# Scores of the last 64 queries of two heads as four fp32 matmuls on 64x64 tiles, and a new order of all rounds

## The chip, the cores and the metric

The kernel runs on one core of one Trainium2 chip. The time is that of the device for one execution, in microseconds (us), as the median of the runs shown. Work is done by TensorE (PE in the rows; its weight loads are PEld), VectorE (DVE), ScalarE (ACT) and GpSimd (POOL); SyncE (SP) issues most of the DMAs. Each of them runs its own instructions in the order in which the program lists them, and waits where an operand or a buffer is not ready yet.

## What is computed

Attention with a bias that depends on the positions, and after it a feed-forward layer with a softplus. The shapes are B = 4, H = 8, S = 576, D = 64, and for the layer 2304 tokens, 512 columns in and out and 2048 hidden.

```python
def _attn_ref(q, k, v, w1, b1, w2):
    scores = np.matmul(q, k.transpose(0, 1, 3, 2)) / np.sqrt(D)
    rel = (pos[:, None] - pos[None, :]).astype(np.float32)
    x = (np.log1p(np.abs(rel)) / np.log1p(np.maximum(pos[:, None], 1.0)))[..., None]
    bias = np.maximum(x @ w1 + b1, 0.0) @ w2
    scores = scores + bias.transpose(2, 0, 1)[None]
    attn = np.exp(scores - np.max(scores, axis=-1, keepdims=True))
    attn = attn / (np.sum(attn, axis=-1, keepdims=True) + 1e-09)
    return np.matmul(attn, v)

def _moe_ref(x, w_in, w_out):
    h = x @ w_in
    return (np.maximum(h, 0.0) + np.log1p(np.exp(-np.abs(h)))) @ w_out
```

## The kernel before

The first part (to about 66 us) computes the bias tables of all heads and, between them, the scores of the first two units. A **unit** n (16 of them) is one batch element and a pair of heads; the second part works through them in **rounds** 0 to 15, and in round n it multiplies the probabilities of unit n with v, while it makes the scores of unit n+1 and splits the q and k of unit n+2. The third part (from about 320 us) is the feed-forward layer.

Two heads have 2 x 576 query rows, which make nine tiles of 128 rows: tiles 0 to 3 are of the first head, 5 to 8 of the second, and tile 4 holds the last 64 queries of both. q and k come into the tiles `qn` and `kn` (pool `nat`, two buffers each; `kn` holds k twice, once in each half of the partitions). VectorE or ScalarE round them to fp32r (`hi_q`, `hi_k`, into `qq` and `kk`), and GpSimd subtracts to get what the rounding left out (`lo_q`, `lo_k`). A tile's scores are four matmuls of 128x288: two halves of the keys, each with the high and the low part of k, and the contraction over 128 partitions adds the high and the low part of q. Tile 4 takes eight, because the two heads are added up in one accumulation: in `qq` 64 columns of zeros lie between the two heads' queries, so that the product of the other head's rows is zero.

The order within a round is written out by hand, in strings of tokens (`ROUND0`, `ROUND1`, `ROUND` for rounds 2 to 13, `ROUND14`, `ROUND15`). A token is an instruction group of one engine, and a letter behind a slash names the engine of a copy (a for ScalarE, d for VectorE):

- `S4` is the matmuls of the scores of tile 4 of unit n+1, into one of two PSUM buffers `s` in turn (`Z4` the same for unit n). `A4` adds the bias and finds the row's extreme, on VectorE, and frees the buffer. `X4` is the exponential with the row's sum, on ScalarE.
- `T31` is the transposes of part 1 of key block 3 of unit n, into one of two PSUM buffers `t` in turn (three transposes; `T40` two, of the key tail's copies `tl`). `V31` copies them to SBUF and frees the buffer. `L0` to `L4` make the tail copies, on GpSimd.
- `P0` to `P4` multiply key blocks 0 to 4 with v, on TensorE in fp32, where each matmul leaves two records in the trace. P0 to P3 use array tiles of 128x64, and P4, the key tail, four of 64x64. P3 and P4 of unit n-1 stand at the head of round n.
- `I` adds up and inverts the row sums, `R` transposes them, `C` copies them and sends them out to memory, from where they come back spread over 64 partitions (`rb`); `O` multiplies the product with them.
- `Kh`, `Qh0`, `Qh1` are the roundings of k and of the two heads' q, `Kl`, `Ql0`, `Ql1` the subtractions.
- `B0` to `B4` decode a block of the layer's weights: B0 on ScalarE, B1 on GpSimd, B2 to B4 on VectorE.

The loads (`LOADS`) are hung on the numbers of tokens in the round.

Of the kernel before, what the change touches and what calls it, by code (L numbers as in the profile page):

```python
# [42 lines left out]


ROUND = """
Qh1/d Kh/a P3 P4 T20 T02 S2 Qh0/a I V20/d V02/d T11 V11/a A2 S3 T12 V12/a T00 V00/a S7 A3 O T10
A7 V10/a S4 R Kl S0 X3 C B0 T41 T22 Ql1 V41/a A4 S1 V22/a B1 A0 Ql0 T30 V30/a S6 T01 T21 V01/a
X7 S5 A1 B2 X4 A6 V21/d T31 V31/d X2 S8 A8 T32 X0 A5 B3 X8 L0 V32/d X5 X1 T40 P0 L2 L1 P1 V40/d
L4 P2 X6 L3 B4
"""  # L50

ROUND0 = """
Z7 T20 T30 V20/a A1 A0 ZA7 V30/a ZX7 Z3 X1 A6 X0 Z4 ZA3 A2 Z8 T10 ZX3 ZA8 ZX8 T00 A5 V00/d ZL2
ZL1 V10/d T40 T12 T02 X6 V40/a V12/a A7 ZA4 X7 A3 V02/a T32 ZX4 V32/d T22 V22/a X2 I T01 R Qh1/d
ZL3 T31 ZL4 V01/a C A4 T11 X5 P0 Kh/a X4 V11/d Qh0/d L2 Ql0 Kl X3 L1 L4 A8 L0 P1 X8 V31/d T21 L3
V21/d T41 V41/d P2 Ql1
"""
# [64 lines left out]
def tile_log_bias_attention__then__softplus_ffn(  # L122
# [192 lines left out]
    def u_split(n):  # L315

        def hi_k(on="d"):
            kk[n] = kp.tile([128, 2, 2, S], F32R, tag="kk", name="kk")
# [6 lines left out]
        def hi_q(i, on="d"):  # L330
# [1 line left out]
            copy_on(on, qq[n % 2][up, 640 * i:640 * i + S], q_n[n][up])

        def lo_q(i):
            done.add(("q", n, i))
            qt = qq[n % 2][:, 640 * i:640 * i + S]
# [1 line left out]
            sub_on(n)(qt[down], q_n[n][up], qt[up], op=ALU.subtract)
# [24 lines left out]
    def u_s(n, t):  # L363

        pr, b = divmod(n, B)
        st_ = {}

        def pe():
            ssum[n] = sums[n % 3]
            if t == 4:  # L370
# [10 lines left out]
            if t < 4:  # L381
                terms = [(0, 128 * t)]
            elif t > 4:
                terms = [(1, 128 * t + 64)]
            else:
                terms = [(0, 512), (1, S)]
            for half in range(2):
                for i, (hd, c0) in enumerate(terms):
                    for j in range(2):
                        nc.tensor.matmul(  # L390
                            ps[:, half, :SH],
                            lhsT=qt[:, c0:c0 + 128],
                            rhs=kt[:, hd, j, half * SH:half * SH + SH],
                            start=(i == 0 and j == 0),
                            stop=(i == len(terms) - 1 and j == 1),
                        )
# [692 lines left out]
```

## Time and profile before

| | |
|---|---|
| time, median of 3 runs (lowest to highest) | 710.72 us (710.49 to 710.92) |
| the profiled execution | 713.52 us |
| its span, first to last instruction | 711.7 us |
| busy in the span: PE, PEld | 684.4 us, 538.2 us |
| busy in the span: DVE, ACT, POOL | 526.7 us, 532.6 us, 122.1 us |
| mean granted clock of TensorE | 0.990 |

The profiled execution took 1.8 us more than its span and 2.8 us more than the median. Steps are costed in its span; what they change is then taken from the median. A record of a matmul is longer than its place in the stream, because matmuls are pipelined: 288 columns show as some 295 ns, though the next one starts 133 ns later. How long TensorE is held is read from the distance between starts.

### The profile page before, as it was taken

To read this page: it belongs to the slowest core of one execution; us is meant where nothing else is said; L and a number is where in the kernel's file an instruction comes from. 1 tells how busy PE (TensorE), PEld (TensorE's weight loads), DVE (VectorE), ACT (ScalarE), POOL (GpSimd) and SP (SyncE) were. 2 spreads that over 40 slices of the span, in tenths; PEclk is the share of its full clock that TensorE was granted. 3 is DMA by queue.
4 is the path that set the end of the run, shared out by engine and by line. 5 is a ranking of instruction groups with operands and counts; after the bars stand their busy time and mean duration, and the time that the engine had idled before them with its cause. 6 is when DMAs were issued, how large, how long until landed. Compare 5 with 4: busy or idle time off the path is not lost.

```text
span 711.7 us, 11929 instructions
## 1 busy us (share of the span) xinstructions
PE 684.4 (96%) x4128; PEld 538.2 (76%) x4128; DVE 526.7 (74%) x1115; ACT 532.6 (75%) x1079; POOL 122.1 (17%) x150
## 2 busy tenths in 40 slices
PE   5689899999999999999999999999999999999997
PEld 2135588877888777757888888888888888888886
DVE  6996788887888887767968695678695554666464
ACT  6989788888888887778777686777677665665654
POOL 0000555455655454210000000000000000000000
PEclk9999899999999999999999999999999999999999
DMA  5866786677677543555232120512020220412221
GB/s 139 305 225 218 245 295 209 215 245 237 190 227 229 168 144 112 161 164 175 93 144 75 50 99 1 178 65 84 29 75 16 103 75 1 137 41 81 68 80 39
DMA packets 51036, 96.76 MB, mean 136 GB/s; under 512 B 7440, under 2 KB 15008, under 8 KB 50976
## 3 DMA queue, kind: packets, MB, share of 16 engines
q1 hardware_dynamic: 50460, 95.41, 41.0%
q8 instruction: 32, 0.52, 0.3%
q10 hardware_dynamic: 516, 0.60, 0.2%
q14 instruction: 28, 0.23, 0.1%
HBM read 67.98 MB, written 28.01 MB: 135 GB/s over the span
## 4 chain that ended last, share of the span: by engine, by line
PE 85%; ACT 5%; DMA 4%; DVE 4%; issue 1%; SPq 0%; ACTq 0%; POOL 0%; POOLq 0%; DVEq 0%
PE y L854 28%; PE h L796 27%; PE s L390 10%; PE o L504 10%; PE t L467 6%; PE acc L232 3%; DVE p L406 2%; DMA e_d<-e 2%; ACT p L422 2%; DVE b L689 1%; ACT e L253 1%; PE t L475 1%; DMA a<-w_d 1%; DMA r_d<-r 1%; DMA dist<-in_c_dist_dram 1%
## 5 line engine op out<-in xcount | busy, mean ns | idle before, releaser
L796 PE MATMUL h<-x,wi 128*128 128x512 f32 (+1 forms) x960 | 212.4, 370 | 1.1 <-DVE wi L769 1.1
L854 PE MATMUL y<-wo,g 128*128 128x512 f32 x864 | 209.8, 391 | 0.0
L796 PEld LDWEIGHTS h<-x,wi 128*128 128x128 f32 x960 | 169.1, 189 | 35.1 <-DVE wi L769 1.8
L854 PEld LDWEIGHTS y<-wo,g 128*128 128x128 f32 x864 | 161.2, 188 | 33.7 <-DVE g L828 0.2
L819 DVE SCALAR_TENSOR_TENSOR u<-u,e 128x512 f32<-128x512 f32 (+1 forms) x80 | 50.9, 637 | 102.3 <-ACT l L816 102.0
L390 PE MATMUL s<-kk,qq 128*128 128x288 f32 x640 | 118.0, 315 | 1.1 <-ACT p L400 0.2
L406 DVE CUSTOM_DVE_ANT_0 p<-s,b 128x576 f32<-128x576 f32 x135 | 99.5, 753 | 17.1 <-PE s L390 16.6
L422 ACT ACTIVATE p<-p,m 128x576 f32<-128x576 f32 x144 | 109.7, 765 | 3.1 <-DVE b L695 2.5
L812 ACT ACTIVATE e<-h 128x512 f32<-128x512 f32 (+1 forms) x80 | 44.2, 553 | 76.5 <-PE h L796 76.5
L390 PEld LDWEIGHTS s<-kk,qq 128*128 128x128 f32 x640 | 90.2, 191 | 9.6 <-DVE m L406 5.0
L467 PE MATMUL t<-ident,p 128*128 128x128 f32 x576 | 89.2, 280 | 1.8 <-ACT pt L355 1.6
L355 ACT ACTIVATE pt<-t 128x384 f32<-128x384 f32 (+1 forms) x126 | 58.3, 488 | 36.4 <-PE t L467 34.8
L504 PE MATMUL o<-pt,vn 128*64 128x256 f32 (+3 forms) x640 | 78.6, 416 | 0.0
L467 PEld LDWEIGHTS t<-ident,p 128*128 128x128 f32 x576 | 66.7, 142 | 14.3 <-issue 7.9
L504 PEld LDWEIGHTS o<-pt,vn 128*64 128x64 f32 (+1 forms) x640 | 38.9, 137 | 32.0 <-issue 5.7
L826 ACT ACTIVATE g<-l 128x512 fp32r<-128x512 f32 (+1 forms) x80 | 46.8, 586 | 20.4 <-DVE l L823 10.6
L357 DVE COPY pt<-t 128x384 f32<-128x384 f32 (+1 forms) x98 | 48.5, 530 | 15.8 <-PE t L467 15.6
L439 POOL COPY tl<-p 128x128 f32<-128x128 f32 x80 | 30.8, 399 | 146.2 <-ACT p L422 139.7
L232 PE MATMUL acc<-m,coef 128*32 128x512 f32 (+17 forms) x352 | 37.9, 528 | 17.6 <-ACT e L253 10.3
L828 DVE TENSOR_TENSOR g<-l,g 128x512 fp32r<-128x512 f32 (+1 forms) x80 | 50.3, 628 | 3.7 <-ACT g L826 3.7
L823 DVE TENSOR_TENSOR l<-l,u 128x512 f32<-128x512 f32 (+1 forms) x80 | 50.4, 630 | 0.0
L821 DVE SCALAR_TENSOR_TENSOR l<-h,l 128x512 f32<-128x512 f32 (+1 forms) x80 | 50.4, 630 | 0.0
(56 smaller groups left out, 686.1 us busy)
## 6 DMA issues: line engine op xcount, KB each, us to landing
e_d<-e SPq DMA_DIRECT2D x36, 295.5 KB, 5.0
kn<-in_k_dram SPq DMA_DIRECT2D x16, 576.0 KB, 4.9
b<-e_d SPq DMA_DIRECT2D x32, 288.0 KB, 4.4
r<-in_moe_w_in_dram SPq DMA_DIRECT2D x16, 512.0 KB, 3.5
r<-in_moe_w_out_dram SPq DMA_DIRECT2D x16, 512.0 KB, 3.6
xr<-x_d SPq DMA_DIRECT2D x28, 256.0 KB, 3.4
vn<-in_v_dram SPq DMA_DIRECT2D x16, 320.0 KB, 8.5
qn<-in_q_dram SPq DMA_DIRECT2D x16, 288.0 KB, 4.7
```

Of the source, the lines that this page charges most:

```text
L232: nc.tensor.matmul(acc[32 * g:32 * g + 32, lo:hi], lhsT=coef.rearrange("p o h -> p (o h)"), rhs=hid[s, g][:, lo:hi], start=True, stop=True ...
L355: nc.scalar.activation(dst, src, AF.Copy)
L390: nc.tensor.matmul(ps[:, half, :SH], lhsT=qt[:, c0:c0 + 128], rhs=kt[:, hd, j, half * SH:half * SH + SH], start=(i == 0 and j == 0), stop= ...
L406: nc.vector.tensor_tensor_reduce(prob[n, t].rearrange("p (a c) -> p a c", a=2), st_["ps"][:, :, :SH], bias[pr, t].rearrange("p (a c) -> p ...
L422: nc.scalar.activation(p, p, AF.Exp, bias=st_["m"], scale=-1.0, accum_out=ssum[n][:, PLACE.index(t):PLACE.index(t) + 1],)
L467: nc.tensor.transpose(ps[:, 128 * i:128 * i + 128], prob[n, t][:, 128 * jb:128 * jb + 128], ident,)
L504: nc.tensor.matmul(o[up, half, 0:w], lhsT=v_n[n][rows, jb, hd], rhs=pt[n, jb][rows, c0:c0 + w], start=(jb == 0), stop=(jb == 4), tile_posi ...
L796: nc.tensor.matmul(ps[:, :nb], lhsT=wi[f][:, a, 128 * c:128 * c + 128], rhs=xs[bi, c][:, x_, :nb], start=(i == 0), stop=(i == 11),)
L819: nc.vector.scalar_tensor_tensor(u, u, -1.0, e, op0=ALU.add, op1=ALU.subtract)
L821: nc.vector.scalar_tensor_tensor(l, ps, 0.0, l, op0=ALU.max, op1=ALU.add)
L823: nc.vector.tensor_tensor(l, l, u, op=ALU.subtract)
L854: nc.tensor.matmul(y, lhsT=g[:, a, 128 * ts:128 * ts + 128], rhs=wo[f][:, w_], start=(first and i == 0), stop=(last and i == 2),)
```

## The change

Tile 4 no longer uses the rounded parts. Its scores are four fp32 matmuls, one for each head and half of the keys, straight from `qn` and `kn`, each on an array tile of 64x64: the half of the keys chooses the half of the partitions, the head the half of the output's partitions. For that the host lays 64 more columns of q out (each half of the partitions then holds the last 64 queries of both heads), `qn` is 640 columns wide, the pool `nat` has three buffers, and the roundings and subtractions of q take 512 columns instead of 576. The zeros in `qq` are gone.

```diff
+            if t == 4:
+                for half in range(2):
+                    rows = slice(64 * half, 64 * half + 64)
+                    for hd in range(2):
+                        c0 = ((512, S), (S, 0))[hd][half]
+                        nc.tensor.matmul(
+                            ps[64 * hd:64 * hd + 64, half, :SH],
+                            lhsT=q_n[n][rows, c0:c0 + 64],
+                            rhs=k_n[n][rows, hd, half * SH:half * SH + SH],
+                            start=True,
+                            stop=True,
+                            tile_position=(64 * half, 64 * hd),
+                        )
+                return
...
-            else:
-                terms = [(0, 512), (1, S)]
...
-            copy_on(on, qq[n % 2][up, 640 * i:640 * i + S], q_n[n][up])
+            copy_on(on, qq[n % 2][up, 512 * i:512 * i + 512], q_n[n][up, 64 * i:64 * i + 512])
...
-                t = nat.tile([128, S], F32, tag="qn", name="qn")
+                t = nat.tile([128, S + 64], F32, tag="qn", name="qn")
...
+NAT = 3
...
-    nat = pool(es_s, "nat", 2, "right")
+    nat = pool(es_s, "nat", NAT, "right")
```

All the strings of tokens are new. In rounds 2 to 13 S4 now stands between P3 and P4; in round 1 it stands behind P4 and T20, and in round 14 between P3 and T20. K's rounding moves from ScalarE to VectorE (`Kh/a` to `Kh/d`) in rounds 2 to 13, and two more of the copies V go to ScalarE (10 of 14, from 8). The order of the loads is new, too. Line numbers shift by up to 14.

On TensorE, the head of a round in the middle of the attention, before: the products P2, P3 and P4 (two rows each), then T20 with T02, and the scores S2. `o` is the product's PSUM tile, `pt` the transposed probabilities, `vn` the values, `t` the PSUM tile of the transposes.

```order
L504 MATMUL o<-pt,vn 64x256 x2
L504 MATMUL o<-pt,vn 64x320 x2
L504 MATMUL o<-pt,vn 64x256 x2
L504 MATMUL o<-pt,vn 64x320 x2
L504 MATMUL o<-pt,vn 64x256 x2
L504 MATMUL o<-pt,vn 64x320 x2
L467 MATMUL t<-ident,p 128x128 x6
L390 MATMUL s<-kk,qq_126 128x288 x4
```

The same place after, with S4 as the row `s<-kn,qn`:

```order
L510 MATMUL o<-pt,vn 64x256 x2
L510 MATMUL o<-pt,vn 64x320 x2
L510 MATMUL o<-pt,vn 64x256 x2
L510 MATMUL o<-pt,vn 64x320 x2
L382 MATMUL s<-kn,qn 64x288 x4
L510 MATMUL o<-pt,vn 64x256 x2
L510 MATMUL o<-pt,vn 64x320 x2
L473 MATMUL t<-ident,p 128x128 x3
L396 MATMUL s<-kk,qq_125 128x288 x4
```

S4 moved to between P3 and P4, and S2 from behind T02 to ahead of it. On TensorE, the place in the middle of the round where S4 stood before: S7, T10, S4 (the row of eight), R (on `ss`, the sums), S0 and T41:

```order
L390 MATMUL s<-kk,qq_126 128x288 x4
L467 MATMUL t<-ident,p 128x128 x3
L390 MATMUL s<-kk,qq_126 128x288 x8
L556 MATMUL t<-ident,ss_128 128x128
L390 MATMUL s<-kk,qq_126 128x288 x4
L475 MATMUL t<-ident,tl 128x128 x3
```

The row of eight is gone from there; after, S7, R, S0 and T10 follow each other.

On VectorE, the last third of the same round, before: A1 (the first pair of rows; `p` the scores with the bias, `m` their extreme), B2 (`b<-a`), A6, the copies V21 and V31 (one row of two), A8, A5, B3 (`b<-r,b`) and V32:

```order
L406 ISA p,m<-s,b 128x576
L406 ISA m 128x1
L689 TENSOR_SCALAR b<-a 128x512
L406 ISA p,m<-s,b 128x576
L406 ISA m 128x1
L357 COPY pt<-t 128x384 x2
L406 ISA p,m<-s,b 128x576
L406 ISA m 128x1
L406 ISA p,m<-s,b 128x576
L406 ISA m 128x1
L695 SCALAR_TENSOR_TENSOR b<-r,b 128x512
L357 COPY pt<-t 128x384
```

The same stretch after, from V30 on: V30, A1, A6, B2, V31, A5, B3 and A8.

```order
L355 COPY pt<-t 128x384
L412 ISA p,m<-s,b 128x576
L412 ISA m 128x1
L412 ISA p,m<-s,b 128x576
L412 ISA m 128x1
L695 TENSOR_SCALAR b<-a 128x512
L355 COPY pt<-t 128x384
L412 ISA p,m<-s,b 128x576
L412 ISA m 128x1
L701 SCALAR_TENSOR_TENSOR b<-r,b 128x512
L412 ISA p,m<-s,b 128x576
L412 ISA m 128x1
```

A6 went ahead of B2. V30 came to VectorE from ScalarE, and V21 went the other way. V31 stands alone, behind A6 and B2. V32 is no longer in this stretch.

On VectorE, the stretch behind it, over the end of the round, before: B4 (`a<-r,b`), the rounding Qh1, the two steps of I (`ss`), and V20 and V02 of the next round:

```order
L700 SCALAR_TENSOR_TENSOR a<-r,b 128x512
L357 CAST qq_124<-qn 64x576
L542 TENSOR_SCALAR ss_128<-ss_128 128x9
L543 RECIPROCAL ss_128<-ss_128 128x9
L357 COPY pt<-t 128x384 x2
```

After: B4, V32, Qh1, Kh, the two steps of I, and A4:

```order
L706 SCALAR_TENSOR_TENSOR a<-r,b 128x512
L355 COPY pt<-t 128x384
L355 CAST qq_124<-qn 64x512
L355 CAST kk<-kn 128x2x576
L548 TENSOR_SCALAR ss_126<-ss_126 128x9
L549 RECIPROCAL ss_126<-ss_126 128x9
L412 ISA p_2307,m<-s,b 128x576
L412 ISA m 128x1
```

V32 is now the last copy of its round, behind B4. Kh came in from ScalarE, where it stood ahead of Qh0, and A4 follows I; V20 and V02 went to ScalarE.

## Rows read from the trace of the kernel before

**Rows 1.** Page, part 4: share of the span in the chain that ended last, by engine

```profile
PE 85%; ACT 5%; DMA 4%; DVE 4%; issue 1%; SPq 0%; ACTq 0%; POOL 0%; POOLq 0%; DVEq 0%
```

**Rows 2.** Busy time by window: length, each engine's busy us, granted clock, DMA share, GB/s

```profile
70.00:80.00 10.00, 7.18 (x35) 4.68 (x35) 7.60 (x21) 9.12 (x24) 1.63 (x4) 0.68 0.94 321
166.50:181.64 15.14, 15.08 (x125) 12.25 (x123) 12.84 (x32) 12.91 (x31) 8.11 (x9) 1.00 0.55 173
```

**Rows 3.** Timeline of PE, mid-round: start us, us, engine, line, operation, tiles, count

```profile
179.06 0.82 PE L467 MATMUL t<-ident,p 128*128 128x128 f32 x6
179.64 0.77 PE L390 MATMUL s<-kk,qq 128*128 128x288 f32 x4
180.25 0.49 PE L467 MATMUL t<-ident,p 128*128 128x128 f32 x3
180.49 1.31 PE L390 MATMUL s<-kk,qq 128*128 128x288 f32 x8
181.66 0.77 PE L390 MATMUL s<-kk,qq 128*128 128x288 f32 x4
```

**Rows 4.** Timeline of PE, end of the same round

```profile
184.89 0.77 PE L390 MATMUL s<-kk,qq 128*128 128x288 f32 x4
185.50 0.49 PE L467 MATMUL t<-ident,p 128*128 128x128 f32 x3
186.07 0.79 PE L390 MATMUL s<-kk,qq 128*128 128x288 f32 x4
```

**Rows 5.** Timeline of PE, products with v, passes taken one by one, then T20

```profile
173.45 0.39 PE L504 MATMUL o<-pt,vn 128*64 128x256 f32 x2
173.67 0.44 PE L504 MATMUL o<-pt,vn 128*64 128x320 f32 x2
173.94 0.44 PE L504 MATMUL o<-pt,vn 128*64 128x320 f32 x2
...
175.88 0.44 PE L504 MATMUL o<-pt,vn 128*64 128x320 f32 x2
176.24 0.50 PE L504 MATMUL o<-pt,vn 64*64 64x256 f32 x4
176.51 0.50 PE L504 MATMUL o<-pt,vn 64*64 64x256 f32 x4
176.94 0.87 PE L467 MATMUL t<-ident,p 128*128 128x128 f32 x6
```

**Rows 6.** Timeline of DVE, end of the same round: A1, B2, A6, V21 with V31

```profile
183.65 0.76 DVE L406 CUSTOM_DVE_ANT_0 p<-s,b 128x576 f32<-128x576 f32 x1 [0.37 <-PE s L390]
184.34 1.00 DVE L689 TENSOR_SCALAR b<-a 128x512 int32<-128x512 int32 x1
185.26 0.74 DVE L406 CUSTOM_DVE_ANT_0 p<-s,b 128x576 f32<-128x576 f32 x1
185.93 1.01 DVE L357 COPY pt<-t 128x384 f32<-128x384 f32 x2
```

**Rows 7.** Timeline of DVE, head of a round: B3, Qh1, V20 with V02

```profile
173.12 0.69 DVE L695 SCALAR_TENSOR_TENSOR b<-r,b 128x512 int32<-128x512 int32 x1
175.23 0.46 DVE L357 CAST qq<-qn 64x576 fp32r<-64x576 f32 x1
177.53 1.02 DVE L357 COPY pt<-t 128x384 f32<-128x384 f32 x2 [0.81 <-PE t L467]
```

**Rows 8.** Timelines of POOL and DVE, Kl, Qh1 and Ql1 in rounds 0, 1 and 7

```profile
81.96 2.64 POOL L328 TENSOR_TENSOR kk<-kn,kk 128x1152 fp32r<-128x1152 f32 x1
83.39 1.52 DVE L357 CAST qq<-qn 64x576 fp32r<-64x576 f32 x1
180.14 1.43 POOL L338 TENSOR_TENSOR qq<-qn,qq 64x576 fp32r<-64x576 f32 x1
```

**Rows 9.** Timeline of ACT, head of a round: the last X, then Kh

```profile
175.41 0.76 ACT L422 ACTIVATE p<-p,m 128x576 f32<-128x576 f32 x1
176.17 1.15 ACT L355 ACTIVATE kk<-kn 128x1152 fp32r<-128x1152 f32 x1
```

More of the change, by code (lines that the diff above doesn't have):

```diff
@@ L45 @@
 ROUND = """
[L46 to L49, printed above, removed]
+B0 Qh1/d Qh0/a P3 S4 P4 T20 V20/a S2 Kh/d T02 I A4 O A2 V02/a T12 S3 V12/a T11 A3 T00 S7 V11/a
+V00/d Ql0 R B1 S0 X3 C A7 T10 T41 A0 V10/a V41/a S1 T30 V30/d Kl A1 T22 X0 S6 V22/a T01 V01/a
@@ L50 @@
+T21 A6 V21/a S5 B2 T31 V31/d T32 S8 X7 T40 A5 B3 X4 V40/a X6 X1 X2 A8 P0 X5 X8 L0 B4 L2 L1 P1 L4
+L3 Ql1 V32/d P2
 """
 ROUND0 = """
[L53 to L56, printed above, removed]
+Z7 T20 T30 V30/a V20/a A1 A0 ZA7 ZX7 A6 X0 A2 Z3 Z4 ZA3 Z8 T10 ZX3 ZA8 ZX8 T00 A5 ZL1 T40 V00/d
@@ L57 @@
+V10/d ZL2 X1 A7 T12 T02 X6 ZA4 V40/a V12/a X7 A3 V02/a ZX4 T32 T22 V22/a V32/d I T01 R T11 ZL4
+V01/a ZL3 T31 C A4 Qh1/d X5 Kh/a X3 V11/d Qh0/d X4 X2 P0 Ql0 Kl A8 L0 P1 X8 L3 V31/d T21 V21/d
+L1 T41 V41/d P2 L4 Ql1 L2
 """
 ROUND1 = """
-Qh1/d Kh/a P3 P4 T20 Qh0/a I T02 S2 T11 V20/d V02/d V11/a A2 S3 T12 V12/a T00 V00/a S7 A3 O T10
-R Ql1 Kl X3 S4 S0 C V10/a T41 T22 B0 A7 V41/a A4 B1 S1 V22/a A0 Ql0 T30 T01 X4 V30/a V01/a S6 X7
-A1 S5 B2 A6 T21 V21/d T31 V31/d S8 A8 B3 T32 X0 A5 T40 X8 P0 X2 X5 X1 L2 X6 L0 L4 V40/d L3 P1 B4
@@ L63 @@
-P2 L1 V32/d
+Qh1/d Kh/a P3 P4 T20 S4 Qh0/a I T11 T02 S2 V20/d V02/d V11/a A4 A2 T12 S3 V12/a T00 V00/a S7 A3
+O T10 R Ql1 Kl X3 S0 V10/a C T41 T22 B0 A7 V41/d S1 V22/a A0 Ql0 T01 B1 X4 T30 V01/a S6 V30/a X7
+A1 B2 A6 S5 T21 V21/d T31 V31/d S8 A8 B3 T32 X0 A5 T40 X8 P0 X2 X5 X1 L0 L2 X6 L4 V40/d B4 P1 L3
+L1 V32/d P2
 """
 ROUND14 = """
-Qh0/d Kh/a P3 Qh1/d P4 I T20 T02 S2 V20/d V02/d T11 V11/a A2 S3 T12 V12/a T00 O V00/a S7 A3 T10
-A7 V10/a R S4 X3 C Kl B0 S0 T41 T22 Ql1 V41/a A4 S1 V22/a A0 T30 A1 V30/a B1 S6 T01 V01/a T21 B2
@@ L69 @@
-S5 A6 V21/d T31 X4 V31/d Ql0 X7 S8 X2 T32 X0 A5 A8 B3 X5 X1 L0 V32/d X8 T40 P0 V40/d P1 L2 X6 B4
-P2 L4 L3 L1
+Qh0/d Kh/a P3 I Qh1/d S4 T20 T02 P4 S2 V20/d A4 V02/d T11 V11/a A2 S3 T12 V12/a T00 O V00/a A3
+T10 S7 A7 V10/a R X3 C Kl B0 S0 T41 T22 Ql1 V41/d V22/a A0 S1 T30 A1 V30/a B1 S6 T01 T21 B2 S5
+A6 V21/d T31 V01/a X4 V31/d Ql0 S8 X7 X2 T32 B3 X0 A5 A8 X5 X1 L0 V32/d X8 T40 P0 V40/d P1 L2 X6
+L4 L3 L1 B4 P2
 """
 ROUND15 = """
-P3 I T00 V00/a T01 P4 T02 V02/a f2 T10 V01/d O R V10/d C T11 V11/a T12 V12/d P0 T32 f0 V32/a T20
@@ L75 @@
-V20/d T21 V21/d T22 P1 f7 T30 f4 f5 V22/a V30/d f3 T31 V31/a T40 f8 V40/a f9 T41 f1 V41/d f10
-f11 B0 P2 f6 B1 B2 B3 B4 f12
+P3 I T00 V00/a f2 T01 P4 V01/d T02 V02/a T10 O R V10/d C T11 V11/a T12 V12/d P0 T32 f0 V32/a T20
+V20/d T22 T21 V21/d P1 f7 T30 f4 f5 V22/a V30/d f3 T31 V31/a T40 f8 V40/a f9 T41 f1 V41/d f10
+f11 B0 P2 B1 f6 B2 B3 B4 f12
 """
@@ L95 @@
 LAG_S = (1, 4)
-LOADS = {30: "b", 2: "k", 6: "q", 10: "v", 14: "b", 18: "b", 22: "b", 26: "b", 40: "w"}
-LOADS0 = {74: "w", 14: "k", 35: "v1", 56: "v", 4: "q"}
+LOADS = {22: "b", 4: "q", 0: "v", 34: "w", 6: "k", 25: "b", 23: "b", 10: "b", 31: "b"}
+LOADS0 = {17: "k", 28: "v1", 71: "w", 6: "q", 59: "v"}
 PRE = [(f, i) for f in range(8) for i in range(2)][:15]
@@ L115 @@
 STAGE = """
-21:D00 22:R15 25:R10 25:R16 26:R12 26:D01 27:D05 29:R17 31:R11 32:D02 33:R13 33:D06 33:R18
+21:D00 21:R15 24:R16 25:R10 26:R12 26:D01 27:D05 29:R17 31:R11 31:R13 32:D02 33:D06 33:R18
 34:R14
@@ L262, in tile_log_bias_attention__then__softplus_ffn @@
     N = 16
-    QW = S + 64 + S
     qq = []
     for i in range(2):
-        t = sp.tile([128, QW], F32R, name=f"qq{i}")
-        nc.gpsimd.memset(t[:, S:S + 64].bitcast(F32), 0.0)
-        qq.append(t)
+        qq.append(sp.tile([128, 1024], F32R, name=f"qq{i}"))
     sums = [sp.tile([128, 128], F32, name=f"ss{i}") for i in range(3)]
@@ L331, in hi_q @@
             up = slice(64 * i, 64 * i + 64)
[L332 removed]
+            copy_on(on, qq[n % 2][up, 512 * i:512 * i + 512], q_n[n][up, 64 * i:64 * i + 512])
         def lo_q(i):
             done.add(("q", n, i))
[L336 removed]
+            qt = qq[n % 2][:, 512 * i:512 * i + 512]
             up, down = slice(64 * i, 64 * i + 64), slice(64 - 64 * i, 128 - 64 * i)
[L338 removed]
+            sub_on(n)(qt[down], q_n[n][up, 64 * i:64 * i + 512], qt[up], op=ALU.subtract)
         return hi_k, lo_k, hi_q, lo_q
@@ L378, in pe @@
             st_["ps"] = ps
+            if t == 4:
[12 more added lines that the diff above has]
+                return
             assert all(("q", n, i) in done for i in range(3))
             qt, kt = qq[n % 2], kk[n]
[L381 to L384, printed above, removed]
-            else:
-                terms = [(0, 512), (1, S)]
-            for half in range(2):
[L388 to L396, printed above, removed]
+            hd, c0 = (0, 128 * t) if t < 4 else (1, 128 * t - 128)
+            for half in range(2):
+                for j in range(2):
+                    nc.tensor.matmul(
+                        ps[:, half, :SH],
+                        lhsT=qt[:, c0:c0 + 128],
+                        rhs=kt[:, hd, j, half * SH:half * SH + SH],
+                        start=(j == 0),
+                        stop=(j == 1),
+                    )
         def raw():
@@ L1043, in _lay @@
         else:
-            a[:, 1::2] = np.concatenate([a[:, 1::2, :, 512:], a[:, 1::2, :, :512]], axis=3)
+            e, o = a[:, 0::2], a[:, 1::2]
+            ends = e[..., 512:], o[..., 512:]
+            a = np.stack(
+                [
+                    np.concatenate([e, ends[1]], axis=3),
+                    np.concatenate([ends[1], o[..., :512], ends[0]], axis=3),
+                ],
+                axis=2,
+            ).reshape(B, H, D, S + 64)
     elif name == "v":
```

## The prediction, made before the change was timed

> **What bounds the kernel now.** I read the chain that ended last first: it runs through TensorE for 85% of the span [rows 1]. Next the table by windows. From one R to the next, a round in the middle of the attention takes 15.14 us; TensorE is busy 15.08 of it at the full clock, VectorE 12.84, ScalarE 12.91, GpSimd 8.11 [rows 2]. So in rounds 2 to 13 the time is what TensorE is held for. At the start it is not: between 70 and 80 us TensorE is busy 7.18 of 10 at a granted clock of 0.68, and ScalarE 9.12 [rows 2].
>
> "Busy" hides waits, because a record lasts longer than its place in the stream. So I took the distances between starts. Six transposes and four score matmuls are 1.19 us apart from the next (179.06 to 180.25), three transposes and four matmuls 0.85 (179.64 to 180.49) [rows 3]. That makes three transposes 0.34 and the four matmuls of a tile 0.52. At the end of the round the same pair takes 1.18, from 184.89 to 186.07 [rows 4]: TensorE loses 0.33 us ahead of S8. Who holds it: S8 takes the PSUM buffer of S6, which A6 frees; A6 ran from 185.26 to 186.00 behind the bit step B2 (184.34 to 185.26) [rows 6], and S8 began 0.07 after A6's end. So a round is some 14.8 us of work and 0.33 of waiting.
>
> **What goes.** S4's eight matmuls: from 180.49 to S0 at 181.66 is 1.17 [rows 3], with R's one transpose (0.11, a third of 0.34) in it, so 1.06 us per unit.
>
> **What comes.** No score matmul on a 64x64 tile in fp32 is in the trace, but P4 is the same form with other widths. An fp32 matmul leaves two passes. In P1, 256 columns hold the array 0.22 us and 320 hold it 0.27 [rows 5], so 288 hold it some 0.24. Do four tiles run side by side? P4's first four passes, 256 and 320 wide, stand in one row from 176.24, its second four in one from 176.51, and T20 follows at 176.94 [rows 5]: 0.70 for eight passes that one after the other would be 1.96. So S4 is two passes, 0.48 us. A change of tile shape costs: P3's last 320 columns begin at 175.88 and P4 at 176.24, 0.36 instead of 0.27, and the first weights are not hidden, which makes P4's first pass 0.27 instead of 0.22 [rows 5]; 0.15 together. In rounds 2 to 13 S4 lies between P3 and P4, both changes are there already, and S4 costs its 0.48 alone: 1.06 - 0.48 = **0.58 us less work** per round. In rounds 1 and 14 transposes lie between S4 and P4, which is two more changes, 0.30, and leaves 0.28. The bounds: the passes hidden beside P3 and P4 altogether (0, a gain of 1.06), and the tiles two by two (0.96, a gain of 0.10). I take 0.48, since P4's rows are the nearest. Z4 and the first unit's tile 4 lie where ScalarE and VectorE bound, and gain nothing.
>
> **What the order moves.** On VectorE A6 now goes ahead of B2, and S8 no longer waits: **0.33 less**. But V31 now stands behind A6 and B2, and T40 needs the PSUM buffer that V31 frees, since the two buffers alternate (T31, T32, T40). I add both ways up from T30's end. A copy starts 0.2 after its transposes (T20 from 176.94 takes 0.34 and its first weights 0.05; V20 begins at 177.53 [rows 5, 7]). On VectorE: 0.2, V30 0.50 (half of 1.01), A1 0.69, A6 0.69, B2 0.92, V31 0.55 to its end, 0.07 to TensorE's start [rows 6]: 3.62 us. On TensorE: T22, S6, T01, T21, S5, T31, T32, S8, which is five times 0.34 and three times 0.52 [rows 3]: 3.26. T40 would wait **0.36 more**, and with it everything behind on TensorE, P0 to P3 first. VectorE has to be free when T30 ends; it is, since the step ahead, A0 of 0.69, needs only S0, which ends 1.5 us earlier. The bounds for this wait are 0 (if TensorE has lost as much elsewhere in that stretch) and 0.6 (if the tails of the copies add a quarter again).
>
> V32 comes last now, behind A5, B3, A8 and B4. From V31's end to its end that is 0.69 for each of the four, and 0.5, 3.26 at most; P3 begins 0.23 (T40), 0.1 and three times 0.97 behind T40's start, 3.24 in all, and T40 itself starts 0.07 behind V31's end. Its second matmul needs V32. The slack is 0.05, so no cost in the sum, and up to 0.2 for the range.
>
> K's rounding leaves ScalarE (1.15 there [rows 9]), and with it two copies V come in, so ScalarE ends its round no later. In the new order the copies V20, V02, V12 and V11 each end when the transposes that need their buffer come up, some with no slack that I can read; up to 0.25 per round goes into the range, 0 into the sum. The roundings and subtractions of q shrink by a ninth, on engines that wait anyway: nothing. The wider loads of q and the third buffer: a unit's q and k are loaded two rounds ahead, so S4 does not wait for them, and the longer life of `kn` and `qn` is covered by the buffer. On SP the loads of v, q and k come behind the write of the weights' block; two rounds of lead cover that.
>
> **The sum.** Rounds 2 to 13: 12 x (-0.58 - 0.33 + 0.36) = 12 x -0.55 = -6.6. Rounds 1 and 14: -0.56. Round 0 and the first part: 0, with 1 us either way, as the clock there is low. The feed-forward part starts when the attention ends and is carried along. Together -7.2: the span goes from 711.7 to 704.5, the profiled execution from 713.5 to 706.3. The median of the runs is 2.8 below the profiled one, so **703.5 us**.
>
> **Rivals.**
> - *No new wait.* T40's wait does not appear. Then a round saves 0.91, and the time is 710.7 - 10.9 - 0.6 = 699.2. For it: 0.36 is the difference of two sums of seven terms. Against: each of these terms is a row.
> - *More waits.* ScalarE's copies and V32 cost the bounds above, 0.25 per round: 703.5 + 3.0 = 706.5. For it: VectorE and ScalarE would be at 88% of a 14.6 us round. Against: both have free stretches in the product's part of the round.
> - *The tiles don't run side by side.* S4 takes 0.96, the round saves 0.07, and rounds 1 and 14 lose 0.2 each: 710.3, no change. P4's rows speak against it.
> - *Slower: K's rounding on VectorE is caught by GpSimd.* In round 1 a rounding of 64x576 took 1.52 us while GpSimd's Kl ran (81.96 to 84.60); it ended 0.3 after Kl [rows 8]. Undisturbed, the same takes 0.46 [rows 7]. In the new order GpSimd's Ql1 (1.43 [rows 8]) follows the last tail copy, which waits for X8. By my sums X8 ends 4.5 us behind T40's start (V40, then five X of 0.76 [rows 9]), so Ql1 runs from about 4.8 to 6.2; Kh can begin at about 3.8. One us later, and it waits for Ql1 to end. I and A4, behind it in the queue, would come 2.3 later, S3, for which A4 frees the buffer, has 1.4 of slack, and with A2 behind O the round loses some 1.2: 12 x (1.2 - 0.55) - 0.6, so 718. It decides from a VectorE that is 1 us late at Qh1. The Trainium skill (SBUF — State Buffer, section "SBUF: two separate sides") says that VectorE and GpSimd share a pair of ports under an exclusive lock, and whoever comes first keeps it for a whole instruction. The 1.52 us row agrees; by that rule a rounding that starts first is safe.
>
> **How the numbers follow.** The forecast (702 to 705) has 0.50, no new wait 0.15, more waits 0.22, the tiles in turn 0.05, slower 0.08. A measurement of this kernel can tell 0.2%, 1.4 us, from no change. Faster: the first three, 0.87; same: 0.05; slower: 0.08. To hold 8 in 10, the range takes in the first three with the end of the second one's bounds: 699.0 to 708.0.
>
> **What would show it.** In the profile after: four rows' worth of 64x64 passes between P3 and P4, two starts some 0.24 us apart, and P4 right behind without a change of shape; S8 0.85 behind the start of the pair ahead of it, T40 some 0.36 late, with V31 just ahead of it on VectorE behind B2; R to R some 14.6 us in rounds 2 to 13; the roundings on VectorE at 0.75 or less each. I am wrong if S4's passes start one behind the other, if a round stays over 15 us, if P3 waits for V32, or if a rounding lasts over 1 us in these rounds.

## The result, and the profile after

The changed kernel takes 702.33 us (median of four runs, 701.86 to 702.75), the kernel before beside it 710.82 (710.49 to 712.87). The ratio is 0.9874, with a 95% interval of 0.9855 to 0.9894: 8.5 us faster. The forecast was 703.5, so the time and the direction came out as foretold. Two of the steps under it did not, and their errors partly cancel.

The profiled execution of the changed kernel took 702.75 us, its span 700.9. The chain that ended last runs through TensorE for 88%, before for 85% [rows 1]. By windows (length, each engine's busy us in the order of [rows 2], granted clock, DMA share, GB/s), the stretch after 70 us and one round, from R to R:

```profile
70.00:80.00 10.00, 7.90 (x45) 5.06 (x46) 7.56 (x21) 8.66 (x23) 2.87 (x5) 0.83 0.96 333
161.04:175.36 14.32, 14.32 (x124) 11.49 (x123) 12.32 (x32) 12.54 (x32) 7.32 (x10) 1.00 0.81 273
```

A round went from 15.14 us [rows 2] to 14.32, 0.82 less, and TensorE's records now fill it. From the R of round 2 to the R of round 13, eleven such rounds take 157.56 us, before 166.59: 9.0 less. From there to the R of round 15 it is the other way: 27.94, before 27.30, 0.6 more. From that R to the end nothing changes (411.75, before 411.93). 9.0 less 0.6 is 8.4, near the difference of these medians (8.5); for a second pair of medians further down it is 9.6. Of the 0.6, 0.33 is no loss: in the new order T10 stands behind R and not ahead of it, so behind the R of round 13 the changed kernel has three transposes of `p` more (69 where there were 66), and ahead of the R of round 2 three less. The S4 of round 2 lies ahead of its R in both kernels, so what it gains is not in these stretches either. What lies ahead of round 2 differs from one execution of the same kernel to the next by as much as it differs here (last section), so it is in no sum.

TensorE at the head of a round, passes one by one as in [rows 5]: P3's last, S4 twice (L382), P4 twice, T20.

```profile
170.52 0.44 PE L510 MATMUL o<-pt,vn 128*64 128x320 f32 x2
170.89 0.47 PE L382 MATMUL s<-kn,qn 64*64 64x288 f32 x4
171.18 0.42 PE L382 MATMUL s<-kn,qn 64*64 64x288 f32 x4
171.42 0.45 PE L510 MATMUL o<-pt,vn 64*64 64x256 f32 x4
171.64 0.50 PE L510 MATMUL o<-pt,vn 64*64 64x256 f32 x4
172.07 0.55 PE L473 MATMUL t<-ident,p 128*128 128x128 f32 x3
```

Four tiles stand in one row, so they run side by side, and S4 is two passes, 0.29 and 0.24 us apart from what follows. The change of shape ahead of it is 0.37 from P3's last start, as it was ahead of P4 (175.88 to 176.24 [rows 5]), and P4's first pass now holds the array 0.22 instead of 0.27. From P3's last start to T20 it is 1.55, before 1.06: S4 costs 0.49.

TensorE at the end of the same round, which answers to [rows 4]: T01 with T21, S5, T31 with T32, S8, T40, and the first of P0.

```profile
178.40 0.84 PE L473 MATMUL t<-ident,p 128*128 128x128 f32 x6
179.03 0.80 PE L396 MATMUL s<-kk,qq 128*128 128x288 f32 x4
179.67 0.82 PE L473 MATMUL t<-ident,p 128*128 128x128 f32 x6
180.24 0.79 PE L396 MATMUL s<-kk,qq 128*128 128x288 f32 x4
180.86 0.39 PE L481 MATMUL t<-ident,tl 128*128 128x128 f32 x2
181.18 1.19 PE L510 MATMUL o<-pt,vn 128*64 128x256 f32 x8
```

S8 follows its six transposes after 0.57 us: its wait of 0.33 is gone. S5 has a small new one (0.63 after six transposes). T40 comes 0.62 after S8, right behind it: the forecast wait of 0.36 is not there. VectorE in the same stretch tells why: V30, A1, A6, B2 (L695), V31, and then the end of the round, V32, Qh1 and Kh.

```profile
177.75 0.56 DVE L355 COPY pt<-t 128x384 f32<-128x384 f32 x1 [0.74 <-PE t L473]
178.22 0.75 DVE L412 CUSTOM_DVE_ANT_0 p<-s,b 128x576 f32<-128x576 f32 x1
...
178.89 0.75 DVE L412 CUSTOM_DVE_ANT_0 p<-s,b 128x576 f32<-128x576 f32 x1
...
179.57 0.42 DVE L695 TENSOR_SCALAR b<-a 128x512 int32<-128x512 int32 x1
180.20 0.56 DVE L355 COPY pt<-t 128x384 f32<-128x384 f32 x1 [0.20 <-PE t L473]
...
183.23 0.55 DVE L355 COPY pt<-t 128x384 f32<-128x384 f32 x1
183.81 0.42 DVE L355 CAST qq<-qn 64x512 fp32r<-64x512 f32 x1
184.27 0.76 DVE L355 CAST kk<-kn 128x1152 fp32r<-128x1152 f32 x1
```

B2 takes 0.42, where it took 1.00 [rows 6], and V31 waits 0.20 for its transposes instead of being late itself. On GpSimd, nothing runs beside B2 any more. Its last subtraction ahead of B2, Kl, ends at 177.60, 1.97 us before B2 begins:

```profile
174.94 2.66 POOL L326 TENSOR_TENSOR kk<-kn,kk 128x1152 fp32r<-128x1152 f32 x1
```

In the trace of the kernel before, the same instruction stands at both lengths. These are the last two of the attention on VectorE (L689):

```profile
275.20 0.98 DVE L689 TENSOR_SCALAR b<-a 128x512 int32<-128x512 int32 x1
...
290.45 0.42 DVE L689 TENSOR_SCALAR b<-a 128x512 int32<-128x512 int32 x1
```

and this is Ql0 on GpSimd in that kernel, beside the first of them:

```profile
274.48 1.42 POOL L338 TENSOR_TENSOR qq<-qn,qq 64x576 fp32r<-64x576 f32 x1
```

Ql0 runs until 275.90, and the first B2 ends 0.28 later. In round 14 there is no q left to split, and GpSimd has no subtraction beside the second. So the result raises one theory above the others: the wait of 0.33 ahead of S8 came from **GpSimd holding B2 up**, and not from B2's place ahead of A6.

### The profile page after: what moved, and what is told of

It is laid out like the page before. It is cut to its first block, busy times and chain, and to the rows that moved or that the text cites. A ratio compares the mean times of both kernels' runs of the same rounds, so it can differ in the third digit from the quotient of the medians.

```text
span 700.9 us, 11869 instructions
## 1 busy us (share of the span) xinstructions
PE 673.1 (96%) x4128; PEld 524.4 (75%) x4128; DVE 520.8 (74%) x1105; ACT 527.9 (75%) x1089; POOL 111.6 (16%) x148
## 4 chain that ended last, share of the span: by engine, by line
PE 88%; DMA 4%; ACT 3%; DVE 2%; issue 1%; SPq 1%; POOL 0%; ACTq 0%; POOLq 0%; DVEq 0%
PE y L860 28%; PE h L802 27%; PE s L396 9%; PE o L510 9%; PE t L473 8%; PE acc L233 4%; ACT e L254 2%; DMA e_d<-e 2%; PE s L382 1%; PE t L481 1%; DMA rb<-r_d 1%; DMA tab<-in_c_tab_dram 1%; ACT p L428 1%; DMA b<-e_d 0%; DMA a<-w_d 0%
## 5 line engine op out<-in xcount | busy, mean ns | idle before, releaser
L396 PE MATMUL s<-kk,qq 128*128 128x288 f32 x512 | 97.4, 317 | 1.2 <-DVE m L412 0.9
L353 ACT ACTIVATE pt<-t 128x384 f32<-128x384 f32 (+1 forms) x148 | 66.9, 480 | 32.0 <-PE t L473 31.8
L473 PE MATMUL t<-ident,p 128*128 128x128 f32 x576 | 85.4, 279 | 2.2 <-ACT pt L353 1.4
L396 PEld LDWEIGHTS s<-kk,qq 128*128 128x128 f32 x512 | 72.3, 190 | 9.1 <-issue 2.3
L355 DVE COPY pt<-t 128x384 f32<-128x384 f32 (+1 forms) x76 | 41.6, 552 | 17.4 <-PE t L473 17.0
L445 POOL COPY tl<-p 128x128 f32<-128x128 f32 x80 | 24.9, 341 | 167.3 <-ACT p L428 167.2
```

Source lines behind the costliest of these rows:

```text
L396: nc.tensor.matmul(ps[:, half, :SH], lhsT=qt[:, c0:c0 + 128], rhs=kt[:, hd, j, half * SH:half * SH + SH], start=(j == 0), stop=(j == 1),)
L473: nc.tensor.transpose(ps[:, 128 * i:128 * i + 128], prob[n, t][:, 128 * jb:128 * jb + 128], ident,)
```

## The experiments

Ratios are against the kernel before, timed beside each of them (median 711.6 to 711.8). A round is the median time from R to R in rounds 2 to 12.

**Ql0 out of B2's way, nothing else.** In the row of tokens of rounds 2 to 13 of the kernel before:

```diff
-... A4 S1 V22/a B1 A0 Ql0 T30 ...
+... A4 S1 V22/a Ql0 B1 A0 T30 ...
```

> The kernel before with one token moved: in rounds 2 to 13 GpSimd's Ql0 goes ahead of B1 instead of behind it. Nothing else changes. In the trace of before, B2 on VectorE takes 0.98 to 1.00 us in every round in which Ql0 runs beside it, and 0.42 where it does not. Theory 1 (B2 is held up by GpSimd's subtraction, and S8 waits for A6 behind it): B2 takes 0.42, A6 begins some 0.6 earlier, S8 no longer waits, a round goes from 15.14 to some 14.82, and the time from 710.7 to some 707 (12 rounds and 0.32). Theory 2 (B2 is long by itself there, and only the order of A6 and B2 matters): B2 stays at 1.0, a round at 15.14, the time at 710.7.

Measured: 707.37 us, ratio 0.9938 (0.9917 to 0.9959), a round of 14.80 instead of 15.14. B2 in rounds 3 to 12 (instances, then ns as minimum, median and maximum):

```profile
L689 DVE TENSOR_SCALAR b<-a x10: 421/423/423, 123.4 to 256.5; 128x512 int32<-128x512 int32 x10
```

The order of VectorE is untouched, A6 still stands behind B2, and the wait is gone all the same. Of the 0.82 us, 0.34 is this.

**The new form of S4 in its old place.** The changed kernel's matmuls, layout of q and buffers, with the strings of tokens and the order of the loads of the kernel before (of the diff, the rows of rounds 2 to 13):

```diff
-B0 Qh1/d Qh0/a P3 S4 P4 T20 V20/a S2 Kh/d ...
+Qh1/d Kh/a P3 P4 T20 T02 S2 Qh0/a I V20/d ... T10 A7 V10/a S4 R Kl S0 X3 C B0 T41 ...
```

> The new form of the scores alone (fp32 on 64x64 tiles, q laid out with 64 more columns, three buffers), with all strings of tokens, loads and stages of the kernel before: S4 stays alone between T10 and R. By the prediction's terms S4 costs 0.48 and two changes of tile shape of 0.15 each, against 1.06: a round loses 0.28 of 15.14, if S8's wait of 0.33 stays as it is, and the time goes to some 707. Theory 2, the tiles do not run side by side when other shapes stand on either side: S4 takes 0.96 and 0.3, a round gets 0.2 longer, the time 713.

Measured: 709.85 us, ratio 0.9969 (0.9955 to 0.9982), a round of 14.97: 0.17 less, not 0.28. TensorE's timeline: T10, S4, R, S0.

```profile
192.26 0.49 PE L473 MATMUL t<-ident,p 128*128 128x128 f32 x3
192.68 0.71 PE L382 MATMUL s<-kn,qn 64*64 64x288 f32 x8
193.32 0.33 PE L562 MATMUL t<-ident,ss 128*128 128x128 f32 x1
193.49 0.80 PE L396 MATMUL s<-kk,qq 128*128 128x288 f32 x4
```

From T10 to S0 it is 1.23, before (180.25 to 181.66 [rows 3]) 1.41. So a lone S4 takes 0.88 where the eight matmuls took 1.06. Its two passes are 0.49 of it, and the changes of shape on both sides 0.39: the prediction had 0.30 for them.

**The new place as well.** The same kernel, with S4 between P3 and P4 and A4 ahead of A2, and everything else in the old order:

```diff
-... P3 P4 T20 T02 S2 ... T11 V11/a A2 S3 ... V10/a S4 R ... V41/a A4 S1 ...
+... P3 S4 P4 T20 T02 S2 ... T11 V11/a A4 A2 S3 ... V10/a R ... V41/a S1 ...
```

> As e2_form, and in rounds 2 to 13 S4 moves to between P3 and P4, and A4 ahead of A2; the rest of the order is that of before. Theory 1 (S4 lies within a shape that is there anyway): a round is 0.3 shorter than in e2_form, some 14.56, with S8's wait of 0.33 still in it, and the time some 703.5. Theory 2 (the place does not matter, since weights are loaded beside the matmuls): a round as in e2_form, 14.86.

Measured: 724.28 us, ratio 1.0179 (1.0156 to 1.0202), a round of 16.29. Neither theory had this. TensorE, T11 and then S3:

```profile
183.64 0.50 PE L473 MATMUL t<-ident,p 128*128 128x128 f32 x3
184.73 0.53 PE L396 MATMUL s<-kk,qq 128*128 128x288 f32 x2 [0.59 <-DVE m L412]
```

and VectorE: V20 with V02, then A4.

```profile
182.98 1.02 DVE L355 COPY pt<-t 128x384 f32<-128x384 f32 x2 [1.35 <-PE t L473]
183.92 0.75 DVE L412 CUSTOM_DVE_ANT_0 p<-s,b 128x576 f32<-128x576 f32 x1
```

S3 takes the buffer that A4 frees. A4 could have run in the 1.35 us in which VectorE waits for T20, but stands behind the copies; S3 begins 0.83 late.

**Both.** The last kernel with Ql0 out of B2's way.

```diff
-... V22/a B1 A0 Ql0 T30 ...
+... V22/a Ql0 B1 A0 T30 ...
```

> As e3_place, and Ql0 ahead of B1 as in e1_ql0. If the two gains add up (0.58 from the scores, 0.32 from S8's wait), a round takes some 14.24 and the time is some 700, below the changed kernel's 702.3, whose round 14 became longer. If the rest of the new order is needed as well, a new wait shows in the round, and it stays at 14.5 or above.

Measured: 720.49 us, ratio 1.0131 (1.0105 to 1.0158), a round of 15.89. Ql0's place is worth 0.40 here, but the loss stays.

**A4 ahead of the copies.**

```diff
-... S2 Qh0/a I V20/d V02/d T11 V11/a A4 A2 S3 ...
+... S2 Qh0/a I A4 V20/d V02/d T11 V11/a A2 S3 ...
```

> The kernel e4_both with A4 moved on VectorE: ahead of the copies V20 and V02 instead of behind them. In e4_both VectorE idles 0.95 us ahead of V20, A4 frees the scores' buffer late, and S3 waits 0.83 us on TensorE, T41 behind it another 0.65; a round takes 15.89. Theory 1, what S4's new place needs is A4's place and nothing else of the new order: S3's wait goes, T41's with it, a round takes 14.4 to 14.6 and the time is 701 to 705. Theory 2, the copies V20 and V02 have to leave VectorE as well, since A2 and A3 queue behind them: S3's wait goes, but A3 stays late and T41 goes on waiting 0.65 or more, so a round takes 15.0 to 15.2 and the time is some 710 to 712. Theory 3, A4 isn't it: 15.5 or more.

Measured: 710.61 us, ratio 0.9981 (0.9964 to 0.9997), a round of 15.04. S3's wait is gone, which is 0.85 of the loss, so A4's place is what S4's place needs first. What is left lies on T41 and T22 in the middle of the round (TensorE, in their order):

```profile
180.59 0.52 PE L481 MATMUL t<-ident,tl 128*128 128x128 f32 x3
181.41 0.55 PE L473 MATMUL t<-ident,p 128*128 128x128 f32 x3 [0.30 <-ACT r L566]
```

ScalarE at that time, V10, X3 and C:

```profile
179.96 0.49 ACT L353 ACTIVATE pt<-t 128x384 f32<-128x384 f32 x1 [0.32 <-PE t L473]
180.34 0.77 ACT L428 ACTIVATE p<-p,m 128x576 f32<-128x576 f32 x1
...
181.10 0.25 ACT L566 ACTIVATE r<-t 9x128 f32<-9x128 f32 x1
```

The size is Theory 2's, its reason is not: X3 is behind V10 on ScalarE, and had not waited for A3.

**C ahead of X3.** In the last kernel:

```diff
-... R Kl S0 X3 C B0 T41 T22 Ql1 V41/a ...
+... R Kl S0 C X3 B0 T41 T22 Ql1 V41/a ...
```

> The kernel e7_a4 with C ahead of X3 on ScalarE, one swap in its row of tokens. In e7_a4 a round takes 15.04 us; T41 begins 0.20 late (its buffer is freed by V10) and T22 behind it 0.46 late, and what T22 waits for is C, which stands on ScalarE behind V10 and X3 (180.34 to 181.10). In the kernel before, S4's 1.06 us of TensorE stood between T10 and T41, and neither waited. Theory 1, S4 in its old place was the cover of that chain on ScalarE, so with C ahead of X3 the 0.46 goes and 0.20 stays: a round of 14.55 to 14.6, some 705. Theory 2, the lateness is VectorE's (the copies V20 and V02, and A3 behind them), and X3, C and T22 wait for it in any order: 14.9 to 15.05, some 710.

Measured: 709.80 us, ratio 0.9987 (0.9968 to 1.0007), a round of 15.03. T22 no longer waits, but the next transposes, T30, do, for the copy V41 on ScalarE:

```profile
181.10 0.55 PE L473 MATMUL t<-ident,p 128*128 128x128 f32 x3 [0.36 <-ACT pt L353]
```

ScalarE there (C, X3, B0, and V41 with V22):

```profile
179.11 0.25 ACT L566 ACTIVATE r<-t 9x128 f32<-9x128 f32 x1
179.26 0.76 ACT L428 ACTIVATE p<-p,m 128x576 f32<-128x576 f32 x1
...
180.02 0.65 ACT L689 ACTIVATE a<-r 128x512 f32<-128x512 f32 x1
180.58 0.83 ACT L353 ACTIVATE pt<-t 128x384 f32<-128x384 f32 x2
```

The size is Theory 2's again, its reason is not: A3 had ended 1.31 us before X3 began (177.96 and 179.26), so it is not VectorE, and it is not C's place. As these rows read, the whole stretch of ScalarE, V10, C, X3, B0, V41, has to fit between T10 and T30. With S4 in its old place 1.06 us of matmuls stood in it, 0.88 in the new form. The changed kernel has taken B0 (0.65) out of the stretch, to the head of the round. That this is what makes its middle free of waits wasn't tried.

**GpSimd back under B2.** The changed kernel with one more subtraction on GpSimd, behind A1, whose result nobody uses:

```diff
-... V30/d Kl A1 T22 X0 S6 ...
+... V30/d Kl A1 G T22 X0 S6 ...
...
+    dump = sp.tile([64, 512], BF16, name="dump")
...
+        elif kind == "G":
+            p = prob[n + 1, 1][0:64, 0:512]
+            nc.gpsimd.tensor_tensor(dump, p, p, op=ALU.subtract)
```

> The changed kernel, with one subtraction of 64x512 more on GpSimd per round, laid so that it runs while VectorE does B2 (its result is used by nobody). In the changed kernel B2 takes 0.42 us and T40 doesn't wait; the kernel before it had a subtraction of GpSimd beside it and took 0.98 to 1.00. Theory 1, GpSimd holds B2 up: B2 takes about 1.0 again, V31 behind it ends about 0.55 later, T40 waits 0.3 to 0.4 us, a round goes from 14.32 to about 14.65 and the time from 702.3 to about 706.5. Theory 2, B2's length comes from its place behind A1 in the kernel before, not from GpSimd: B2 stays at 0.42, the round at 14.32, the time within 0.2%.

Measured: 703.23 us, ratio 0.9874 (0.9847 to 0.9901), a round of 14.37 (one of the eleven took 14.64). The time can't be told from the changed kernel's. B2 on VectorE:

```profile
180.65 0.80 DVE L699 TENSOR_SCALAR b<-a 128x512 int32<-128x512 int32 x1
```

GpSimd's subtraction beside it:

```profile
180.13 1.03 POOL L651 TENSOR_TENSOR dump<-p 64x512 bf16<-64x512 f32 x1 [1.38 <-DVE m L413]
```

The cause is confirmed: the same instruction in the same place takes 0.42 or 0.80 by what GpSimd does. The subtraction had begun half a microsecond before B2, so it held B2 up less than in the kernel before. V31 no longer waits for its transposes, and T40 and P0 are 0.09 late together: the forecast wait exists, but with B2 0.38 longer it has only just begun.

**Twice as much of it.**

```diff
-            nc.gpsimd.tensor_tensor(dump, p, p, op=ALU.subtract)
+            for _ in range(2):
+                nc.gpsimd.tensor_tensor(dump, p, p, op=ALU.subtract)
```

> The changed kernel, with two subtractions of 64x512 more on GpSimd per round instead of e5_under's one, so that GpSimd stays busy while VectorE does B2. In e5_under the one took 1.03 us, ended in the middle of B2, B2 took 0.80 and T40 was 0.09 us late. Theory 1, the chain A1, A6, B2, V31, T40 with B2 held up to the end of GpSimd's instruction: B2 takes 1.0 us or more, each 0.1 us above 0.80 is 0.1 us more of waiting for T40, so with B2 at 1.0 a round takes 14.55 to 14.6 and the time some 3 us more than the changed kernel's. Theory 2, T40 has slack that e5_under didn't use up: a round stays under 14.45.

Measured: 702.20 us, ratio 0.9866 (0.9845 to 0.9886), a round of 14.37 (again one of 14.64), B2 at 0.80 in all of them. B2 ended 0.28 after the first subtraction and the second couldn't hold it, so this doesn't tell how late T40 comes when B2 takes 1.0: that stays open.

**The order of rounds 2 to 13 in round 14.**

```diff
 ROUND14 = """
-Qh0/d Kh/a P3 I Qh1/d S4 T20 T02 P4 S2 V20/d A4 ...
+B0 Qh1/d Qh0/a P3 S4 P4 T20 V20/a S2 Kh/d T02 I A4 ...
```

> The changed kernel, with the order of rounds 2 to 13 in round 14 too, where the tokens of k and q do nothing. In the changed kernel rounds 13 to 15, from R to R, take 27.94 us, 0.63 more than before, with waits of some 0.75 us on TensorE's transposes. Theory 1, the loss is made by round 14's own order (its S4 stands alone between P3 and T20, and its copies come late): these waits go and the time falls by about 1.2 us, to about 701. Theory 2, the last rounds are bound by something that the order doesn't touch (the end of the scores, ScalarE's row of exponentials): no change, within 0.4 us.

Measured: 703.17 us, ratio 0.9881 (0.9854 to 0.9908): no change against the changed kernel. From the R of round 13 to that of 15 it takes 27.20, 0.74 less, but from there to the end 414.78, 3.03 more. That is a loss of 2.3 in the profiled execution; its time shows less, because its R of round 2 came 1.88 earlier than the changed kernel's (101.82 and 103.70). ScalarE's first rounding of the next layer's weights waits for its load:

```profile
288.03 0.63 ACT L773 ACTIVATE wi<-a 128x512 fp32r<-128x512 f32 x1 [3.39 <-DMA a<-w_d]
```

V02 stands behind it, and TensorE's transposes behind V02 begin after 2.16 us of idling, and they are then 0.21 apart instead of 0.11: the granted clock from 289 to 292 was 0.50, the lower of its two levels, 1.2 GHz.

```profile
289.09 1.54 PE L473 MATMUL t<-ident,p 128*128 128x128 f32 x6 [2.16 <-ACT pt L353]
```

The loads (`xr` and `a`) stand on SP behind the write of the weights' block, which waits for B4; in the order of round 14 they are ahead of it. SP's queue in this kernel:

```profile
281.70 0.33 SPq L727 DMA_DIRECT2D w_d<-a  x1
282.13 1.34 SPq L784 DMA_DIRECT2D xr<-x_d  x3
283.52 0.90 SPq L745 DMA_DIRECT2D a<-w_d  x2
```

and in the changed kernel:

```profile
280.94 1.47 SPq L784 DMA_DIRECT2D xr<-x_d  x3
282.45 0.90 SPq L745 DMA_DIRECT2D a<-w_d  x2
285.56 0.32 SPq L727 DMA_DIRECT2D w_d<-a  x1
```

**That rounding out of V02's way.** The last kernel, with f2 (the rounding) later in round 15:

```diff
-P3 I T00 V00/a f2 T01 P4 V01/d T02 V02/a ... T12 V12/d P0 T32 f0 V32/a T20
+P3 I T00 V00/a T01 P4 V01/d T02 V02/a ... T12 V12/d P0 T32 f2 f0 V32/a T20
```

> The kernel e6_r14 with the first weights' rounding of the feed-forward layer on ScalarE (f2) moved in round 15 from ahead of the copy V02 to behind V11. In e6_r14 round 14 gained 0.74 us, but in round 15 that step waited 3.4 us for its load, V02 stood behind it, and TensorE idled 2.2 us and then ran at half clock for 3 us. Theory 1, the load's lateness cost no more than V02's place behind it: the wait and the half clock go, and the time is some 2.5 us under e6_r14's, 700 to 701, under the changed kernel's 702.3. Theory 2, the load itself bounds the end, and whatever needs it next waits instead: no change against e6_r14, 703.

Measured: 700.91 us, ratio 0.9849 (0.9825 to 0.9872). For the comparison the changed kernel ran once more on the same chip:

> The changed kernel once more, on the same chip as e8_end and e9_long, for the comparison: 702 to 703 us, a round of 14.32.

Measured: 701.97 us, ratio 0.9864 (0.9844 to 0.9883), a round of 14.32. In the kernel with f2 moved the stall is gone, and f2 waits only 0.22 for its load.

The R of round 15 comes 2.28 us earlier than in the changed kernel's second profile, but the end only 0.82. In round 15 TensorE then waits longer for copies: one row of twelve transposes takes 2.90 from its start to the next where it took 2.00. And 1.07 of the 2.28 lies ahead of the R of round 2 (101.73 and 102.80); counted from there, this kernel is 0.25 slower to the end (597.39 and 597.14). The median is 1.06 us under the changed kernel's, and the intervals overlap. It is the fastest of these kernels by its median; that it beats the changed kernel isn't shown.

**The kernel before, a second profile.**

> The kernel before, a second profile. The first profiled execution took 713.5 us, 2.8 above the median, and had a stretch of low granted clock of 6.8 us from 73.7 us. If that stretch varies from execution to execution, this one shows it shorter or elsewhere, with a round of 15.14 as in the first; if it belongs to the kernel, it shows again at the same place and length.

Measured: 711.40 us, span 709.6. A round takes 15.16, 0.01 more than in the first profile, and eleven of them 166.73. The stretch after 70 us:

```profile
70.00:80.00 10.00, 6.97 (x48) 4.25 (x48) 8.02 (x22) 9.36 (x24) 3.32 (x5) 1.00 0.96 338
```

There is no low clock in it, where the first profile had 0.68 [rows 2]. The R of round 2 came at 103.90, in the first profile at 105.91: this stretch belongs to the execution, not to the kernel.

## Why the prediction was right, and which of its steps were not

**TensorE bounds the rounds: right.** Its chain share rose, and the 0.82 us that a round lost all show as distances between its starts.

**S4 at 0.48: right.** It measured 0.49, side by side and with both changes of shape already there. The rival in which the tiles run one after the other falls with the first row of four.

**S8's wait of 0.33: right that it goes, the cause was wrong.** "Behind the bit step B2" is what the rows say. But I took B2's 0.92 to be B2's own time. It was Ql0's: with Ql0 moved by two tokens the wait went, with A6 still behind B2. The rows for it were in the trace before the change (0.98 with Ql0 beside it, 0.42 without), and so was the pattern, since I had found a rounding that GpSimd held up for 1.52 [rows 8] and made a rival of it for Kh, but didn't ask it of B2. The Trainium skill (SBUF — State Buffer, section "SBUF: two separate sides"), named there, says it of VectorE's steps in a two-port mode or with two inputs in SBUF. In its direction the trace agrees for B2 and the rounding, and with one thing less: B2, once GpSimd was done, took 0.28 and not its whole 0.42. Not every step is held up. From 106 to 260 us in the kernel before, the A steps and the copies V, which read PSUM, lasted as long beside a subtraction (0.74 to 0.76 and 0.55 to 0.56) as without one.

**T40's wait of 0.36: the step that failed.** It is the difference of two sums. TensorE's side was 3.26 and measured 3.32 (from T30's end, 177.55, to T40, 180.86). VectorE's side was 3.62, with 0.92 for B2 from its start to the next. The run with GpSimd back under B2, where T40 comes right behind V31, gives its terms: 0.20, V30 0.47, A1 0.67, A6 0.68, B2 0.72, V31 0.55, and 0.06 to TensorE's start, 3.35 together, and T40 and P0 came 0.09 late. In the changed kernel B2 is 0.38 shorter, which makes it 2.97, and V31 waits for T31 instead. With B2 at 0.92 it would be 3.55, 0.23 behind TensorE: an estimate from these rows, as no run had it. So the mechanism was there and the mis-sized term was B2. Neither sign named for the wait came: T40 0.36 late, and a round of some 14.6 us. The rival "no new wait" was right on this: 0.91 per round for it, 0.82 measured, with 0.06 of the rest in S5's wait.

**V32, the copies and Kh: nothing, as the sum had it.** V32 ends at 183.78, and P3 begins at 184.14: 0.36 of slack instead of 0.05, mostly because from V31's end to V32's it took 3.02 and not 3.26. The roundings on VectorE took 0.42 and 0.76. The slower rival needed VectorE 1 us late at Qh1; Kh began 3.41 behind T40, 0.4 earlier than the rival's 3.8. The price of such a mishap is real, however: with S4 moved and the rest of the order left, a round lost 1.15 us and the kernel 12.5, by A4's place on VectorE (0.85 of a round) and then, as the rows read, by ScalarE's stretch around X3. The prediction named the copies' slack as what it couldn't read; the changed order had seen to it.

**Rounds 1 and 14 at -0.28 each: S4 right for 14, its waits left out.** From the R of round 13 to that of 15 lie one S4, round 14's, and the end of round 13. By the prediction's terms that is -0.28 - 0.33 + 0.36 = -0.25. It measured +0.64, and +0.31 without the T10 that is there only because R moved. S4 itself kept to its term: from S4's start to S2's is 2.15 in round 14, before, from P4's start to S2's, 1.33, so S4 costs 0.82; the eight matmuls cost 1.09 there (1.70 with S0, less S0's 0.61), which is 0.27 more. What the sum had put at nothing is waits of the new order of round 14, 0.75 together, on three rows of TensorE's transposes; the longest, of 0.42 (0.25 of it idle), is for a copy of ScalarE's:

```profile
275.83 0.55 PE L473 MATMUL t<-ident,p 128*128 128x128 f32 x3 [0.25 <-ACT pt L353]
```

With the order of rounds 2 to 13 there, 0.74 came back, some 0.33 of it because S4 then stands between P3 and P4 (0.49 instead of 0.82). But then the weights' load came late for round 15, and with its rounding moved other waits took its place, so that no gain of it is shown in the time. Round 1 can't be told from the start's own variation.

**The sum.** Rounds 2 to 12 gave 3.0 us more than forecast (11 times 0.82 instead of 0.55), and the stretch from the R of round 13 to that of 15 0.56 less. The forecast's 0.86 ahead of the R of round 2 (round 2's S4, and round 1) can't be seen. That makes 2.4 us more than forecast; the medians show 1.3 for the first pair (8.5 where 7.2 was forecast) and 2.4 for the second (9.6). That the time came so near to the forecast is in part luck: one error was larger than the other, and the rest lies in what differs between executions. Of the 0.82, Ql0's place is 0.34 and the form of S4 0.17; the other 0.31 is the place between P3 and P4 (0.39 of shape changes saved, less S5's 0.06 and what is too small to name), and none of the kernels got it without moving A4 and, as far as the runs tell, clearing ScalarE's stretch.

## What to carry to other kernels

Ahead of taking an instruction's duration into a sum, look at all its instances: two lengths (0.42 and 0.98 here) can mean that another engine is in it, and for a step of VectorE from SBUF to SBUF the one to look at is GpSimd. Small matmuls on small array tiles are cheap beside others of the same shape (0.49) and nearly as dear as the full ones by themselves (0.88 against 1.06). And work that is moved away from a place was the cover of something there: moved alone it cost 12.5 us, most of it because a buffer came free late; in the changed kernel, whose order also clears the stretch of ScalarE that it had covered, it gained.
